# Start-up evictions moved to VectorE, the first seeding behind the last V matmul, and one late weight load four chunks later

## The chip, the cores and the metric

The kernel runs on one core of one Trainium2 chip. A core has five engines, each with an instruction queue of its own that is worked through in order: TensorE (PE, matmuls, with its weight loads shown as PEld), VectorE (DVE), ScalarE (ACT), GpSimd (POOL) and SyncE (SP, which here only issues DMA transfers). ACT and POOL issue DMA transfers too; an issue stands in the same queue as the engine's other work. Matmul results go to PSUM and are copied from there to SBUF ("evicted") by DVE or ACT. The metric is the device time of one execution in microseconds (us), as the median of several.

## The reference

Two independent parts, whose results stand side by side in the output.

```python
def _A_ref(q, k, v, shift_k, ssm_k, ssm_D):            # S = 2048, D = 1024
    k_shift = sum over t < 4 of k_pad[:, t:t + S] * shift_k[:, 3 - t]
    kv = k_shift * v
    y = irfft(rfft(kv, 2 * S) * rfft(ssm_k, 2 * S))[:S] # a long convolution for each channel
    return q * (y + kv * ssm_D)

def _B_ref(x, mem0, Wq, Wk, Wv, Wo, seg_len):           # 32 heads of 128, 8 memory rows, 64 segments of 32
    mem = mem0
    for s in range(64):
        h = concatenate([mem, x[32 * s:32 * s + 32]])   # 40 rows of 1024
        q, k, v = h Wq, h Wk, h Wv                      # each weight 1024 x 4096
        p = softmax(mask(q k^T * scale))
        o = (p v) Wo                                    # 4096 x 1024
        mem = o[:8]
        outs.append(o[8:])
```

The 64 segments of part B depend on each other through `mem`.

## The kernel before

**Part A** works in three stages: stage 1 makes the shifted product and the first transform, stage 2 (34 units) multiplies the spectra, stage 3 (16 units of y_ps matmuls, an `ot` multiplication on DVE by q, and an output store) transforms back. After each unit of stages 2 and 3 a hook `fill()` is called, which works off a piece of part B's preparation. `units[0]` counts these calls, so it is 34 from the last unit of stage 2 on.

**Preparation of part B.** For the last eight rows of all segments at once, K and Q are made by four dense blocks (`dense`, L616; 16 groups of eight kb_ps matmuls each) and V by two halves of 16 groups (vb_ps, L763). Each group ends in one PSUM tile of the pool `ps0`, which has two, and is evicted by `evac` (L608): two of three by ACT, the third by DVE. A dense block collects in a `stage` tile and goes to the DRAM tensor REC by four stores of 512 KB, issued from ACT's queue (L651). V goes to VBD in eight stores, also from ACT's queue (L766): in its first half from one tile with room for four blocks (`vst`), in its second half from `pair` tiles, of which there are two for four blocks. REC and VBD rows are 256 bytes long in these stores.

**Weights.** They don't all fit in SBUF. Most are resident (Wmid, Wres, Wmore, Wlate, pw, and one called Wring), the others are streamed for each segment from the copy WS through a ring of five slots. All these loads stand in SP's queue in the order of the program; `fetch` (L713) issues the next ring load as soon as `done` (L860) frees a slot. Some resident chunks can be loaded only late, when their place is no longer used by the preparation: `place_late`. Wring is one of them. Its place is that of a `pair` tile, and `done` issues its load at the second streamed chunk of segment 0. Two ring slots lie on the transposed X, which the V matmuls read to the last, and one on the other `pair` tile.

**The segments.** Each projects K, Q and V of its 32 first rows (acc, L938), makes scores, softmax and the attention output, and projects that (yacc, L1029). Before the first segment comes the seeding: the record of segment 0 is loaded from REC (L880), Y is loaded from mem0 (L903), both from POOL's queue; a matmul of zeros clears the score bank SB (L904), the mask is copied into it by DVE (`seed_scores`, L908 and L909), and Y is transposed by PE (`fill_mem`, L885) and copied into the record's tile by DVE (L892).

**Order.** Inside `tc.manual_schedule()`, from L896 on, instructions keep the order of the program. Ahead of it a scheduler puts each engine's instructions in order by its own estimate of when they are ready. An instruction that depends on little may so be drawn ahead: the SB matmul and the eight transposes of the first `fill_mem` stand among the V matmuls in PE's queue, after the second and after the third group. `tc.issue_after(x)` keeps what is traced inside it behind x on x's engine.

Of the kernel before, what the change touches and what calls it, by code (L numbers as in the profile page):

```python
# [30 lines left out]
WO_COPY = 29  # L31
Q_LOAD = (10, 13, 16, 19)
X_LOAD = 1
RING = 5

PITCH = 2048
# [384 lines left out]
def b_kernel(ctx: ExitStack, tc, x, mem0, Wq, Wk, Wv, Wo, outb, n_seg, run_a):  # L421
    nc = tc.nc
# [27 lines left out]
    def dram_chunk(ch):  # L450
        m, a, g = ch
        return Wo_v[a] if m == 3 else W_v[m][a, g]

    def dst_view(ap, ch):
        return ap.rearrange("p (hh d) -> p hh d", hh=2) if ch[0] == 3 else ap

    def stream_src(ch):
        return WS[ring_order.index(ch), :, 0:2048]
# [14 lines left out]
    ident = const.tile([128, 128], BF, name="ident")  # L473
# [7 lines left out]
    def xbt(kc):  # L481
        return XBT[kc // 4][:, kc % 4]
# [3 lines left out]
    def pair():  # L486
        turns["pair"] ^= 1
        return base.tile([128, 2048], BF, tag=f"wring{2 + turns['pair']}", name="pair")
# [7 lines left out]
    def pw(k=None):  # L496
        if k is None:
            k = pw_next[0] % 8
            pw_next[0] += 1
        return pring.tile([128, 2048], BF, tag=f"pw{k}", name="pw")  # L500
# [48 lines left out]
    def make_xbt(su):  # L549
        xb = x.rearrange("(tb s t) d -> tb s t d", s=16, t=SEG)  # L550
        for tb in range(4):
            X_sb = pair()[:, 0:1024]
            with tc.issue_after(su[X_LOAD + tb].ins):
                nc.sync.dma_start(X_sb, xb[tb, :, NX:SEG, :])
# [9 lines left out]
    def group(m, g, temps={}, which=range(8), ws=None, eng=nc.sync, held=False):  # L564
        ws = ws or [None] * 8
        for kc in which:
            ch = (m, kc, g)
            if ch in res:
                got.append(eng.dma_start(res[ch], dram_chunk(ch)))
                ws[kc] = res[ch]  # L570
            else:
                t = temps[ch]() if ch in temps else pw()
                got.append(eng.dma_start(t[:], dram_chunk(ch)))
                if ch in streamed:
                    copies.append((stream_src(ch), t[:]))
                ws[kc] = t[:]
        while copies and not held:
            copied.append(nc.gpsimd.dma_start(*copies.pop(0)))
        return ws
# [4 lines left out]
    def x_load(b):  # L584
        t = base.tile([128, 2048], BF, tag="wring2", name="X_sb")
        x_loads.append(nc.sync.dma_start(t[:].rearrange("p (b d) -> p b d", b=2),
                                         x[b * 128:(b + 2) * 128, :].rearrange("(b p) d -> p b d", b=2)))
        loaded[b], loaded[b + 1] = t[:, 0:1024], t[:, 1024:2048]

    def x_block(b):  # L590
        X_sb = loaded.pop(b)
        if b % 2 == 0:
            t = base.tile([128, 2048], BF, tag="wring3", name="xt")
            xts[b], xts[b + 1] = t[:, 0:1024], t[:, 1024:2048]
        tp = ps0.tile([128, 1024], BF, tag="ps0", name="xt_ps")
        for kc in range(8):
            nc.tensor.transpose(tp[:, kc * 128:(kc + 1) * 128], X_sb[:, kc * 128:(kc + 1) * 128], ident[:])
        xt = xts.pop(b).rearrange("p (s k t) -> p s k t", s=4, k=8)
        rows = tp[:].rearrange("p (k j t) -> p j k t", k=8, j=4)
        nc.vector.tensor_copy(xt[:, :, :, NM:SEG], rows[:, :, :, 0:NX])  # L600
        nc.vector.tensor_copy(xt[:, :, :, 0:NM], rows[:, :, :, NX:SEG])
        rec_stores.append(nc.gpsimd.dma_start(REC[:, 4 * b:4 * b + 4, 0:256], xt.rearrange("p s k t -> p s (k t)")))
# [3 lines left out]
    flip = [0]  # L606

    def evac(dst, src):  # L608
        flip[0] += 1
        if flip[0] % 3:  # L610
            nc.scalar.copy(dst, src)
        else:
            nc.vector.tensor_copy(dst, src)
# [35 lines left out]
    def store():  # L649
        if stores:  # L650
            nc.scalar.dma_start(*stores.pop(0))  # L651

    units = [0]
# [3 lines left out]
    def q1_load(kc, k, ins):  # L657
        res[1, kc, 1] = pw(k)[:]
        with tc.issue_after(ins):
            group(1, 1, which=[kc], ws=q1, held=True)  # L660

    def fill(behind=None):
        store()
        n = units[0]
        units[0] += 1
        if n == 0:
            x_load(0)
        if n >= WO_COPY and wo_copies:
            ch = wo_copies.pop(0)
            with tc.issue_after(rec_stores[-1].ins):  # L670
                nc.gpsimd.dma_start(dst_view(stream_src(ch), ch), dram_chunk(ch))
        if n in Q_LOAD:
            i = Q_LOAD.index(n)
            q1_load(kept_q1[i][1], 4 + i, behind.ins)
        if n > 5 and n % 2 and copies:
            with tc.issue_after(rec_stores[-1].ins):
                copied.append(nc.gpsimd.dma_start(*copies.pop(0)))
        if n % 3 == 2 and blocks:
            b = blocks.pop(0)
            x_block(b)  # L680
            if b % 2 and blocks:
                x_load(b + 1)
        if n >= 34 or n % 3 != 2:
            next(rest, None)

    run_a(ps0, pw, slot16, stage1_done, fill)
# [5 lines left out]
    def more(i):  # L692
        return wres3.tile([128, 2048], BF, tag=f"Wmore{i}", name="Wmore")
# [5 lines left out]
    order_s = [ch for ch in order if ch in streamed]  # L699
# [5 lines left out]
    now = [0]  # L705
# [31 lines left out]
    with c0p:  # L737
        temps = dict(zip(v_temp, homes_v))
        wv = [group(2, 0, temps), None]
        for _ in rest:  # L740
            store()
        wv[1] = group(2, 1, temps)
        for i, ch in enumerate(v_temp):
            if i >= 2:
                home = (lambda i=i: more(i)) if i < len(v_temp) - 2 else (lambda k=i - len(v_temp) + 4: pw(k))
                at_hand[ch] = (wv[ch[2]][ch[1]], home)
        while stores:
            store()
        with tc.issue_after(got[-1].ins):
            for _ in range(2):  # L750
                fetch()
        n_k = len(own[0, 0])
        late = late[n_k:-2] + late[4:n_k] + late[:4] + late[-2:]
        for g in range(2):
            ws = wv[g]
            if g == 0:
                vsts = slot16([128, 4, 4, 512], BF, "vst")
            for tb in range(4):
                vst = vsts[:, tb] if g == 0 else pair()[:].rearrange("p (c w) -> p c w", c=4)
                for c in range(4):  # L760
                    ps = ps0.tile([128, 512], F32, tag="ps0", name="vb_ps")
                    for kc in range(8):
                        nc.tensor.matmul(ps[:], lhsT=xbt(kc)[:, 16 * tb:16 * tb + 16, :].rearrange("p s t -> p (s t)"),  # L763
                                         rhs=ws[kc][:, c * 512:(c + 1) * 512], start=(kc == 0), stop=(kc == 7))
                    evac(vst[:, c, :], ps[:])
                nc.scalar.dma_start(  # L766
                    VBD[16 * tb:16 * tb + 16, :, :, :, g * 128:(g + 1) * 128].rearrange("s t c i e -> (s t) (c i) e"),
                    vst.rearrange("p c (i e) -> p (c i) e", i=4))
            if g == 0:
                with tc.issue_after(got[-1].ins):  # L770
                    place_late(4, stage_home)
                    for i in [*range(len(v_temp) - 2, n_more), *range(len(v_temp) - 2)]:
                        place_late(1, lambda: more(i))
                    place_late(1, lambda: pw(2))
                    place_late(4, stage_home)
        assert len(late) == len(at_hand) + 1
# [10 lines left out]
    SB = ps_s.tile([128, 512], F32, name="SB")  # L787
# [72 lines left out]
    def done(ch):  # L860
        if now[0] == 0 and ch in at_hand:
            place_late(1, at_hand[ch][1])
        elif ch in streamed and (now[0] == 0 or ch not in kept):
            if now[0] == 0 and ch in kept:
                keep(ch)
            free.append(live.pop((now[0], ch))[0])
            if now[0] == 0 and ch == order_s[1]:
                place_late(1, lambda: base.tile([128, 2048], BF, tag="wring2", name="Wring"))
            fetch()

# [2 lines left out]
    P_pad = one.tile([128, 5, 64], BF, name="P_pad")  # L873
# [22 lines left out]
    with tc.manual_schedule():  # L896
        for _ in range(RING - 2):
            fetch()
# [2 lines left out]
        nc.vector.memset(Y[:], 0.0)  # L901
        for dh in range(2):
            nc.gpsimd.dma_start(Y[64 * dh:64 * dh + NM, :], mem0[:, dh * 512:(dh + 1) * 512])  # L903
        nc.tensor.matmul(SB[:, 0:320], lhsT=ident[:], rhs=P_pad[:].rearrange("p b k -> p (b k)"), start=True, stop=True,  # L904
                         skip_group_check=True)

        def seed_scores():
            nc.vector.tensor_copy(S[:, 0:4, :], mask[:, 0:1, :].to_broadcast([128, 4, 40]))  # L908
# [284 lines left out]
```

## Time and profile before

| | us |
|---|---|
| three timed runs | 1820.21, 1822.86, 1832.62 |
| their median | 1822.86 |
| the profiled execution: first to last instruction (span) | 1811.8 |
| PE busy in the span | 1701.8 |
| DVE busy | 1010.3 |
| ACT busy | 680.7 |
| POOL busy | 266.7 |

The page gives the span of the profiled execution, not its time with what lies around it. Times in a row of a timeline are counted from the span's start. A timeline row has start, duration of one or of the merged run, engine (with a q where its sequencer issues a DMA), line, operation, output<-inputs, count, and in brackets how long the engine stood idle before it and what ended that. "PEclk" or "granted clock" is the clock that TensorE was allowed, as a share of full speed.

In 40 equal slices of 45.3 us the page shows where the start-up lies: PE's busy tenths are 6 8 8 8 9 9 6 7 5 9 and then 9 to the end, so segments begin to follow each other without gaps in the eleventh.

### The profile page before, as it was taken

The page shows a single profiled execution, that of the slowest core. Times are in us where ns is not written, and L with a number is a line of the kernel's source. Part 1 is how long each engine was busy: PE and PEld are TensorE (multiplying, and loading weights), DVE is VectorE, ACT ScalarE, POOL GpSimd, SP SyncE. Part 2 cuts the span into 40 slices and gives each one's busy share as a digit, 9 for nine tenths or more (in the row PEclk, how much of TensorE's full clock was granted, in tenths as well). Part 3 has the DMA queues.
Part 4 walks back from the last instruction along what each step waited for, and adds up shares of the span by engine and source line. Part 5 has one row for each costly group of instructions (what it writes and reads, how often), then busy time and mean ns, then how long its engine had stood idle before and what let it go on. Part 6 is the DMA issues. An engine that isn't in the chain of part 4 may idle for free.

```text
span 1811.8 us, 71373 instructions
## 1 busy us (share of the span) xinstructions
PE 1701.8 (94%) x30996; PEld 1000.8 (55%) x31028; DVE 1010.3 (56%) x3391; ACT 680.7 (38%) x1195; POOL 266.7 (15%) x499
## 2 busy tenths in 40 slices
PE   6888996759899999999999999999999999999998
PEld 3443322324566666666666666666666666666665
DVE  9927874201455555555555555555555555555555
ACT  6955651112233333333333333333333333333333
POOL 4003341100111111111111111111111111111111
PEclk9999999889999999999999999999999999999999
DMA  9989889997999999999999999999999999999998
GB/s 340 370 305 305 311 258 320 306 335 210 344 365 361 357 350 360 358 363 353 361 356 358 357 352 360 370 358 360 361 355 362 356 358 366 367 363 356 357 358 300
DMA packets 233070, 623.34 MB, mean 344 GB/s; under 512 B 72802, under 2 KB 72946, under 8 KB 232756
## 3 DMA queue, kind: packets, MB, share of 16 engines
q1 hardware_dynamic: 160948, 550.58, 82.4%
q0 software_dynamic: 17056, 45.13, 7.1%
q10 hardware_dynamic: 54752, 23.07, 4.7%
q8 instruction: 243, 3.98, 0.9%
q14 instruction: 71, 0.58, 0.1%
HBM read 563.63 MB, written 57.67 MB: 343 GB/s over the span
## 4 chain that ended last, share of the span: by engine, by line
PE 77%; DMA 9%; DVE 6%; ACT 4%; issue 3%; ACTq 0%; POOL 0%; SPq 0%; another core or an unknown queue 0%; POOLq 0%; DVEq 0%
PE acc L938 33%; PE yacc L1029 24%; PE kb_ps L622 5%; DMA wring<-WS 4%; PE tps L885 3%; PE tps L957 2%; PE vb_ps L763 2%; ACT OT L1019 2%; DMA REC<-stage 2%; DVE mx L972 1%; DVE E L974 1%; ACT s_sb L247 1%; PE OTp L1007 1%; PE s_ps L245 1%; PE SB L963 1%
## 5 line engine op out<-in xcount | busy, mean ns | idle before, releaser
L1029 PEld LDWEIGHTS <-OT 128*64 128x64 bf16 x8255 | 439.1, 109 | 54.6 <-ACT OT L1019 36.9
L938 PEld LDWEIGHTS <-rec 128*32 128x32 bf16 x12288 | 289.4, 96 | 269.3 <-DVE rec L892 35.2
L947 ACT CAST qkv_sb<-acc 128x512 bf16<-128x512 f32 x384 | 225.1, 586 | 352.2 <-PE acc L938 346.9
L938 PE MATMUL acc<-Wres,rec 128*32 128x512 bf16 x3328 | 240.2, 382 | 2.0 <-issue 1.8
L938 PE MATMUL acc<-wring,rec 128*32 128x512 bf16 x2300 | 229.0, 382 | 8.5 <-DMA wring<-WS 7.3
L1029 PE MATMUL yacc<-Wmore,OT 128*64 128x256 bf16 (+1 forms) x2560 | 220.7, 274 | 0.0
L938 PE MATMUL acc<-Wmid,rec 128*32 128x512 bf16 x3072 | 212.1, 379 | 0.5 <-issue 0.3
L1029 PE MATMUL yacc<-wring,OT 128*64 128x256 bf16 x2448 | 194.9, 273 | 2.7 <-DMA wring<-WS 2.5
L1118 ACT CAST Y<-yacc 128x256 bf16<-128x256 f32 x128 | 47.7, 373 | 269.8 <-DVE quarter_b L795 170.8
L938 PE MATMUL acc<-pw,rec 128*32 128x512 bf16 x1796 | 144.7, 380 | 2.0 <-issue 1.9
L795 DVE TENSOR_SCALAR quarter<-OTp 128x256 int32<-128x256 int32 x252 | 99.9, 418 | 74.3 <-ACT OT L1019 74.3
L1019 ACT CAST OT<-OTp 128x640 bf16<-128x640 f32 x128 | 87.4, 683 | 138.5 <-PE OTp L1011 138.5
L1120 POOL DMA_DIRECT2D out_dram<-Y x128 | 63.9, 503 | 496.3 <-ACT Y L1118 496.0
L892 DVE COPY rec<-tps 128x32 bf16<-128x32 bf16 x128 | 22.4, 175 | 193.6 <-PE tps L885 193.6
L938 PE MATMUL acc<-Wlate,rec 128*32 128x512 bf16 x1536 | 117.3, 379 | 0.1
L1057 DVE COPY KT<-tps 128x512 bf16<-128x512 bf16 x64 | 27.2, 425 | 150.8 <-PE tps L885 150.8
L972 DVE TENSOR_REDUCE mx<-SB 128x8 f32<-128x320 f32 x128 | 63.0, 492 | 78.4 <-PE SB L966 78.4
L880 POOL DMA_DIRECT2D rec<-REC x64 | 36.4, 568 | 453.4 <-PE acc L938 437.9
L977 ACT ACTIVATE E<-E 128x320 f32<-128x320 f32 x128 | 60.1, 469 | 78.3 <-DVE E L974 78.3
L1029 PE MATMUL yacc<-Wlate,OT 128*64 128x256 bf16 x1024 | 79.2, 276 | 6.0 <-issue 0.2
L622 PE MATMUL kb_ps<-XBT,pw 128*128 128x512 bf16 x313 | 81.1, 397 | 2.6 <-DMA pw<-in_B_Wk_dram 1.2
L922 POOL COPY KT<-rec 128x128 bf16<-128x128 bf16 x128 | 38.5, 301 | 253.3 <-PE SB L966 253.3
(224 smaller groups left out, 2627.4 us busy)
## 6 DMA issues: line engine op xcount, KB each, us to landing
wring<-WS SPq DMA_DIRECT2D x831, 512.0 KB, 6.0
wring<-WS SPq DMA_DIRECT2D x64, 384.0 KB, 5.4
rec<-REC POOLq DMA_DIRECT2D x64, 192.0 KB, 5.6
SK<-s_sb SPq DMA_DIRECT2D x16, 512.0 KB, 5.3
SU<-s_sb SPq DMA_DIRECT2D x16, 512.0 KB, 5.6
Kg<-SK SPq DMA_DIRECT2D x32, 256.0 KB, 4.1
Ug<-SU SPq DMA_DIRECT2D x32, 256.0 KB, 5.5
REC<-stage ACTq DMA_DIRECT2D x16, 512.0 KB, 12.9
```

The source lines that it names most:

```text
L622: nc.tensor.matmul(ps[:], lhsT=ws[kc][:, hl * 128:(hl + 1) * 128], rhs=xbt(kc).rearrange("p s t -> p (s t)"), start=(kc == 0), stop=(kc == 7))
L795: nc.vector.tensor_scalar(out=dst, in0=src, scalar1=0, scalar2=None, op0=ALU.bitwise_or)
L885: nc.tensor.matmul(dst[e:e + 32, :], lhsT=src[:, e:e + 32], rhs=ident[:], start=True, stop=True, is_transpose=True, tile_position=(0, e))
L922: nc.gpsimd.tensor_copy(KT[:, :, :, 32:40], KBs[:, 128 * g:128 * g + 128].rearrange("p (c i t) -> p i c t", c=4, i=4))
L938: nc.tensor.matmul(self.acc[32 * c:32 * c + 32, :], lhsT=hT[:, ch[1], :], rhs=w[:, 512 * c:512 * c + 512], start=(ch == chs[0]), stop=(ch ...
L947: nc.scalar.copy(sb[:], self.acc[:])
L972: nc.vector.tensor_reduce(out=mx[:], in_=S, op=ALU.max, axis=AX.X)
L977: nc.scalar.activation(E[:], E[:], ACT.Exp, scale=scale)
L1019: nc.scalar.copy(OT[:], o_view)
L1029: nc.tensor.matmul(yacc[f][64 * dh:64 * dh + m, x - o:y - o], lhsT=lhsT, rhs=r, start=(h == (0, 2 * FIRST[-1])[f] and x == o), stop=stop, ...
L1118: nc.scalar.copy(Y[:, 256 * f:256 * f + 256], yacc[f][:, 0:256])
L1120: nc.gpsimd.dma_start(bass.AP(outb.tensor, outb.offset + SEG * s * 2048 + 512 * dh, [[2048, 32], [1, 512]]), Y[64 * dh + NM:64 * dh + 40, :])
```

## The change

Three parts. Evictions by `evac` go to DVE alone once `units[0]` has reached 34, that is from the last unit of stage 2 through stage 3, the last dense blocks and all of V; ACT keeps the stores. The SB matmul of the seeding is put behind the last V matmul on PE, and with it what follows it in the manual order. Wring's load is issued by `done` at the sixth streamed chunk instead of the second.

```diff
+STAGE3 = 34
+LATE_RING = 5
...
     def evac(dst, src):
         flip[0] += 1
-        if flip[0] % 3:
+        if flip[0] % 3 and units[0] < STAGE3:
             nc.scalar.copy(dst, src)
         else:
             nc.vector.tensor_copy(dst, src)
...
-        if n >= 34 or n % 3 != 2:
+        if n >= STAGE3 or n % 3 != 2:
             next(rest, None)
...
                     for kc in range(8):
-                        nc.tensor.matmul(ps[:], lhsT=xbt(kc)[:, 16 * tb:16 * tb + 16, :].rearrange("p s t -> p (s t)"),
-                                         rhs=ws[kc][:, c * 512:(c + 1) * 512], start=(kc == 0), stop=(kc == 7))
+                        v_last = nc.tensor.matmul(ps[:], lhsT=xbt(kc)[:, 16 * tb:16 * tb + 16, :].rearrange("p s t -> p (s t)"),
+                                                  rhs=ws[kc][:, c * 512:(c + 1) * 512], start=(kc == 0), stop=(kc == 7))
                     evac(vst[:, c, :], ps[:])
...
-            if now[0] == 0 and ch == order_s[1]:
+            if now[0] == 0 and ch == order_s[LATE_RING]:
                 place_late(1, lambda: base.tile([128, 2048], BF, tag="wring2", name="Wring"))
             fetch()
...
-        nc.tensor.matmul(SB[:, 0:320], lhsT=ident[:], rhs=P_pad[:].rearrange("p b k -> p (b k)"), start=True, stop=True,
-                         skip_group_check=True)
+        with tc.issue_after(v_last.ins):
+            nc.tensor.matmul(SB[:, 0:320], lhsT=ident[:], rhs=P_pad[:].rearrange("p b k -> p (b k)"), start=True, stop=True,
+                             skip_group_check=True)
```

In the instruction order of the changed program, PE's 256 V matmuls follow each other and the SB matmul and the transposes stand behind them. DVE has ten dense evictions and 32 of V in one row. In stage 3 some y_ps units and dense groups change places on PE. On SP's queue the load of Wring stands behind four more ring loads, three of them full chunks and one of 384 KB.

## The prediction

> **What bounds the kernel now.** I read the page's head first, then the chain of waits in order of time, then the stretches of the start-up, then each engine's timeline between 300 and 490 us.
>
> ```profile
> span 1811.8 us, 71373 instructions
> PE 1701.8 (94%) x30996; PEld 1000.8 (55%) x31028; DVE 1010.3 (56%) x3391; ACT 680.7 (38%) x1195; POOL 266.7 (15%) x499
> ...
> 365.00:380.00 15.00, 4.80 (x20) 1.81 (x19) 1.25 (x3) 0.00 (x0) 1.25 (x3) 0.85 1.08 380
> 380.00:412.00 32.00, 23.56 (x105) 10.34 (x108) 2.94 (x5) 5.62 (x10) 1.45 (x3) 0.80 1.01 313
> 412.00:441.00 29.00, 27.91 (x129) 12.64 (x130) 3.46 (x5) 6.59 (x12) 0.84 (x2) 1.00 0.67 170
> 441.00:475.00 34.00, 25.34 (x461) 15.43 (x459) 13.49 (x50) 8.35 (x14) 0.85 (x2) 0.90 0.91 324
> ...
> 490.00:511.00 21.00, 20.89 (x463) 13.33 (x460) 12.02 (x48) 7.53 (x14) 2.69 (x6) 1.00 0.97 369
> ```
>
> The span stands for one execution; the median of the timed runs is 1822.86, so 11.1 us lie around the span, and I leave them as they are. Columns of a stretch: length, then busy time of PE, weight loads, DVE, ACT and POOL, the granted clock, the DMA share, GB/s. From segment 1 on PE is busy 20.89 of 21 us: nothing to win there, and the change alters no instruction of those 63 segments. What can be won lies before: from 365 to 412 PE works 28.4 of 47 us, and from 441 to 475, segment 0, it works 25.3 of 34.
>
> ```profile
> 364.70 14.02 DMA REC<-stage
> ...
> 380.38 7.82 DMA Y<-in_B_mem_dram
> ...
> 420.96 9.82 DMA VBD<-pair
> ...
> 441.18 5.16 DMA wring<-WS
> ...
> 453.24 4.20 DMA wring<-WS
> ...
> 464.27 6.13 DMA wring<-WS
> ```
>
> These are links of the chain: start, length, what. PE's own rows say what each link costs:
>
> ```profile
> 371.39 0.81 PE L763 MATMUL vb_ps<-Wres,XBT 128*128 128x512 bf16 x3
> 388.33 0.40 PE L885 MATMUL tps<-ident,Y 128*32 128x128 bf16 x8 [16.14 <-DMA Y<-in_B_mem_dram]
> ...
> 441.63 0.38 PE L763 MATMUL vb_ps<-Wres,XBT 128*128 128x512 bf16 x1
> 442.84 0.40 PE L938 MATMUL acc<-wring,rec 128*32 128x512 bf16 x4 [0.83 <-issue]
> ...
> 446.38 0.40 PE L938 MATMUL acc<-wring,rec 128*32 128x512 bf16 x4 [0.24 <-DMA wring<-WS]
> ...
> 457.49 0.62 PE L938 MATMUL acc<-wring,rec 128*32 128x512 bf16 x4 [5.06 <-DMA wring<-WS]
> ...
> 462.95 0.52 PE L1029 MATMUL yacc<-Wlate,OT 128*64 128x256 bf16 x6
> ...
> 470.44 0.63 PE L1029 MATMUL yacc<-wring,OT 128*64 128x256 bf16 x8 [2.53 <-DMA wring<-WS]
> ...
> 475.09 0.40 PE L938 MATMUL acc<-wring,rec 128*32 128x512 bf16 x4
> ```
>
> Three of 32 V groups (eight matmuls each) are done at 372.2; then PE stands 16.14 us, because the seeding's transposes of Y lie next in its order. V ends at 442.0, segment 1 begins at 475.1. Segment 0 thus takes 33.1 us, with 5.06 and 2.53 us of waits for ring chunks.
>
> **Part 1 and 2: evictions on DVE, seeding behind V.** They have to be costed together.
>
> ```profile
> 364.70 15.98 ACTq L651 DMA_DIRECT2D REC<-stage  x4
> 380.80 1.07 ACT L611 CAST vst<-vb_ps 128x512 bf16<-128x512 f32 x2 [16.13 <-DMA REC<-stage]
> ...
> 369.57 0.69 DVE L613 CAST vst<-vb_ps 128x512 bf16<-128x512 f32 x1 [6.51 <-PE vb_ps L763]
> ...
> 394.29 0.69 DVE L613 CAST vst<-vb_ps 128x512 bf16<-128x512 f32 x1 [5.33 <-PE vb_ps L763]
> 399.47 0.69 DVE L613 CAST vst<-vb_ps 128x512 bf16<-128x512 f32 x1 [4.49 <-PE vb_ps L763]
> ```
>
> ACT issues the four REC stores of the last dense block from 364.70 on and is held by them to 380.68; the V evictions behind them in its queue run at 380.80. With two PSUM tiles, V could not have gone on before about 381.4 even without the seeding. So moving the seeding alone frees 7 us of the 16, moving the evictions alone nothing; together they free all of it. DVE needs 0.69 us an eviction, and a V group comes every 1.73 us (three groups from 394.29 to 399.47), so DVE keeps up, and the 0.10 us by which it is slower than ACT (1.07 for two) stays hidden. With no other wait, 29 groups from 372.2 on end at 372.2 + 29 x 1.73 = 422.4, 19.6 us earlier.
>
> What comes late next is not the weights: the last two chunks for the second half of V are issued at 378.81 (row below), and that half would begin at 372.2 + 13 x 1.73 = 394.7. It is the stores.
>
> ```profile
> 378.81 1.00 SPq L569 DMA_DIRECT2D Wres<-in_B_Wv_dram  x2
> ...
> DMA to landing us min/median/max: 14.2/14.2/14.2
> ...
> DMA to landing us min/median/max: 4.0/4.0/4.0
> ...
> VBD<-vst ACTq DMA_DIRECT2D x4, 512.0 KB, 12.6
> ```
>
> The first landing row is the fourth REC store alone (issued at 378.7, so landed at 392.9), the second the VBD store of 435.8, which ran with hardly a load beside it. ACT's DMA queue is passed in order. In the second half of V two `pair` tiles serve four blocks, so the eviction of block 2 waits until the VBD store of block 0, the fifth in the queue, has landed; before, it had landed at 430.8 (the chain's 420.96 link), about when block 2 came to it. Now V runs 16 us sooner but the REC stores do not. Four REC stores took 364.7 to 392.9, 7.0 us each, beside loads. Up to 412 loads fill the DMA (share 1.01, then 0.67: the stretches above), so I take 7.0 us a store from 392.9: 2.7 stores by 412. The other 2.3 run nearly alone at 4.0 us: 9.2 us. The fifth lands at 421. Then comes the eviction (0.7) and six more groups (10.4): V ends at 432, **9.8 us earlier**. Bounds: stores that cost nothing (422.4, 19.6 us) and every store at the median of 12.6 (a rival below).
>
> The seeding itself now lies between V and segment 0.
>
> ```profile
> 370.17 0.32 DVE L908 CAST SB<-mask 128x160 f32<-128x160 bf16 x1
> 370.53 0.33 DVE L909 CAST SB<-mask 128x160 f32<-128x160 bf16 x1
> 388.78 0.17 DVE L892 COPY rec<-tps 128x32 bf16<-128x32 bf16 x1 [17.93 <-PE tps L885]
> ```
>
> Behind the last V matmul stand on DVE the last eviction (0.69), the two mask copies (0.32 and 0.33) and the copy of the transposed Y (0.17), which the first projection needs: with the small gaps 1.7 us instead of the 0.83 before. The SB matmul and the transposes (0.4 us) run beside the eviction. 0.24 us of the difference disappears in the wait at 446.38. Cost: +0.65 us, between 0 (if the ring chunk lands later anyway) and 0.9. Y and the rec load stay where they are on POOL and land 40 us ahead.
>
> **Stage 3.** There the evictions move behind DVE's `ot` multiplications.
>
> ```profile
> 300.93 2.35 DVE L414 TENSOR_TENSOR ot<-y_ps,qt 128x1024 bf16<-128x1024 f32 x2 [5.70 <-DMA out_dram<-ot]
> ...
> 331.86 1.03 PE L407 MATMUL y_ps<-zt,G2h 128*128 128x512 bf16 x2 [9.04 <-DMA zt<-SZ]
> ```
>
> DVE stands 5.70 us for an output store; two dense groups that ACT evicted meanwhile now wait for it, so that the dense block ends some 2 us later, and with it the REC stores and the zt load behind them. Against it, in the changed order a whole dense group (eight matmuls, 1.7 us) stands ahead of the matmuls of 331.86 and fills part of that 9.04 us wait. I take **0**, between 2 us gained and 2 lost.
>
> **Part 3: the late ring chunk.**
>
> ```profile
> 452.80 0.38 SPq L726 DMA_DIRECT2D Wring<-in_B_Wo_dram  x1
> ...
> 484.00 0.39 PE L938 MATMUL acc<-wring,rec 128*32 128x512 bf16 x4
> ...
> 488.12 0.63 PE L1029 MATMUL yacc<-Wlate,OT 128*64 128x256 bf16 x8
> ```
>
> The load of Wring waits at the head of SP's queue until the last VBD store has landed. Behind it stand the ring chunks whose slots are long free; the chain's 453.24 link is the first of them, and PE waits 5.06 us for it. Four chunks later the same wait stands behind those loads. Its slot comes free between 442.84 and 446.38, when the second ring chunk has been used; issued then, it lands 4.2 to 6.1 us later (the links), so by 452.4, when PE asks. So 5.06 go. The stretch after the wait ran at a lower clock: from 457.49 to 462.95 it took 5.46, in segment 1 (484.00 to 488.12) 4.12: 1.3 us go too. The 2.53 us wait stays, since its chunk can only be loaded when its slot frees. Wring itself is an output chunk, used behind 462.95 and long after its new place. Sum: **-6.4 us**; bounds 0 (chunks late for DMA) and -10.
>
> **Sum.** -9.8 + 0.65 + 0 - 6.4 = -15.5 us: span 1796.3, time 1822.9 - 15.5 = **1807.4**.
>
> **Rivals.** *The stores don't bind* (0.20). If ACT's queue moves the eight VBD stores at the alone price of 4.0 us, the fifth lands by 413 and V ends near 423: 19 - 0.65, with part 3 about 25, 1798. For it: ACT's queue has no evictions between its stores any more. Against: four REC rows at 7.0.
>
> ```profile
> GB/s 415 407 406 409 405 420 309 287 249 301 262 400 408 243 45 289 278 369 390 393 384 342 334 282 206 223 101 133 312 196 310 284 190 163 6 0 211 48 156 314
> ```
>
> This line has the DMA rate in 2 us steps from 364 on: 410 GB/s at its fullest, 45 at 392. From 365 to 475 the four stretches above move 31.7 MB (length times rate); at 380 GB/s, the fullest stretch, that is 83 us, and segment 1 could begin at 448, so DMA as a whole would allow this rival.
> [...]
>
> *Stage 3 gives part of it back* (0.14): DVE's stalls for stores and q loads reach PE through the two PSUM tiles, up to twice the 5.70 us row, and V starts as much later: 4 us gained in all, 1819. Against: PE waits for zt there anyway.
>
> *The stores bind all through* (0.06, the other side). At t us a store from 392.9, the sixth, which the last block waits for, lands at 392.9 + 6t, and V ends 4.2 us later. With 5.7 us gained behind V, it is break-even at t = 8.4. At the median of 12.6, V ends at 472.7: 30.7 - 5.7 = 25 us slower, 1848. For it: the VBD row. Against: those stores came 6.9 us apart (four groups) and so overlapped, and the loads beside them thin out at 412.
>
> That the change does nothing would need the moved instructions to stay in place; in the changed program's order V's 256 matmuls stand together and ACT has no eviction left there.
>
> **How the numbers follow.** The forecast case, 10 to 20 us faster, has 0.60. A measurement of this kernel can tell about 1%, 18.2 us. Faster by more: nearly all of the first rival and a fourth of the forecast, 0.33. Slower by more: the last, 0.06. The same: 0.61. The range reaches from the first rival with part 3 at its bound (1798 - 3.6) to the stage-3 rival with stage 3's own bound on top (1819 + 2): 1794 to 1821. It leaves out the last rival, and the edges of the others.
>
> **What would show it.** Right: no PE wait for Y near 372; V's last matmul between 427 and 436 with its longest wait at block 2 of the second half, put down to VBD<-pair; ACT without an eviction of the dense blocks or of V from stage 3 on; Wring issued behind the 384 KB load, with no 9 us gap of SP ahead; the wait of 5.06 below 2. Wrong: V at 422 or past 440, a ring wait in segment 0 as long as before, or any change of the 20.9 us a segment.

## The result and the profile after

| | before | changed |
|---|---|---|
| median of 12 runs, us | 1822.71 | 1812.70 |
| lowest and highest | 1813.22, 1832.62 | 1807.46, 1817.85 |
| span of the profiled execution | 1811.8 | 1805.7 |

The ratio is 0.9946, with a 95% interval of 0.9926 to 0.9965: 6.4 to 13.5 us faster; the forecast was 15.5. In the profiled executions the difference is 6.1 us. The page and the stretches of the start-up, for the changed kernel:

```profile
span 1805.7 us, 71361 instructions
...
PE 1700.6 (94%) x30996; PEld 999.9 (55%) x31028; DVE 1035.2 (57%) x3429; ACT 658.6 (36%) x1157; POOL 266.1 (15%) x499
```

```profile
365.00:380.00 15.00, 13.17 (x60) 5.85 (x60) 5.54 (x8) 0.00 (x0) 1.14 (x2) 1.00 0.98 373
380.00:412.00 32.00, 31.84 (x147) 14.46 (x148) 12.45 (x19) 0.00 (x0) 2.12 (x4) 1.00 1.07 318
412.00:441.00 29.00, 20.04 (x116) 8.34 (x119) 7.54 (x14) 0.00 (x0) 0.84 (x2) 0.88 0.93 266
441.00:475.00 34.00, 26.26 (x528) 16.36 (x520) 13.22 (x50) 9.79 (x17) 2.69 (x6) 0.90 0.92 336
```

From 365 to 412 PE now works 45.0 of 47 us, where it worked 28.4. ACT has no busy time from 365 to 441: its evictions are gone, the DVE column has grown instead. The stretch behind, 412 to 441, has lost 8 us of PE's work, and the DMA share there rose from 0.67 to 0.93. PE's own rows, of the same kernel, say where it now stands:

```profile
305.36 0.59 PE L599 MATMUL xt_ps<-ident,X_sb 128*128 128x128 bf16 x4 [3.88 <-DVE stage L615]
...
338.90 1.87 PE L409 MATMUL y_ps<-zt,G2h 128*128 128x512 bf16 x4 [9.57 <-DMA zt<-SZ]
...
369.99 0.81 PE L765 MATMUL vb_ps<-Wres,XBT 128*128 128x512 bf16 x3
...
423.99 0.58 PE L765 MATMUL vb_ps<-pw,XBT 128*128 128x512 bf16 x1 [6.85 <-DVE pair L615]
...
434.30 0.38 PE L765 MATMUL vb_ps<-pw,XBT 128*128 128x512 bf16 x1 [0.97 <-DVE pair L615]
...
437.75 0.30 PE L907 MATMUL SB<-P_pad,ident 128*128 128x320 bf16 x1
...
439.37 0.40 PE L941 MATMUL acc<-wring,rec 128*32 128x512 bf16 x4 [1.09 <-DVE rec L894]
...
462.00 1.07 PE L1032 MATMUL yacc<-wring,OT 128*64 128x256 bf16 x8 [4.79 <-DMA wring<-WS]
...
467.35 0.63 PE L1032 MATMUL yacc<-wring,OT 128*64 128x256 bf16 x8 [1.57 <-DMA wring<-WS]
...
470.43 0.40 PE L941 MATMUL acc<-wring,rec 128*32 128x512 bf16 x4
```

The wait of 16.14 us for Y is gone. In its place stands 6.85 us at block 2 of V's second half: DVE's eviction there waits for a `pair` tile, and so for a VBD store. V begins at 369.99 instead of 363.89 and ends near 437.9 instead of 442.0. Segment 0 (439.37 to 470.43) takes 31.1 us where it took 32.25: the wait of 5.06 us for a ring chunk is gone from the projections and is back, with 4.79 us, in the output projection. SP's queue of this kernel, the DMA issues only:

```profile
437.08 8.20 SPq L724 DMA_DIRECT2D wring<-WS  x7
446.50 0.32 SPq L722 DMA_DIRECT2D wring<-WS  x1
454.64 0.38 SPq L728 DMA_DIRECT2D Wring<-in_B_Wo_dram  x1
455.12 0.42 SPq L724 DMA_DIRECT2D wring<-WS  x1
```

The gap of 8 us ahead of Wring has not shrunk with its new place; it stands behind the 384 KB load now. What it waits for is the last VBD store, issued at 438.7. The time from issue to landing of that one store, first in the kernel before (issued at 442.8), then in the changed one:

```profile
DMA to landing us min/median/max: 9.9/9.9/9.9
```

```profile
DMA to landing us min/median/max: 15.9/15.9/15.9
```

### The profile page after: what moved, and what is told of

Read it like the earlier page. It is cut to its first block, busy times and chain, and to the rows that moved or that the text cites. A ratio compares the mean times of both kernels' runs of the same rounds, so it can differ in the third digit from the quotient of the medians.

```text
span 1805.7 us, 71361 instructions
## 1 busy us (share of the span) xinstructions
PE 1700.6 (94%) x30996; PEld 999.9 (55%) x31028; DVE 1035.2 (57%) x3429; ACT 658.6 (36%) x1157; POOL 266.1 (15%) x499
## 4 chain that ended last, share of the span: by engine, by line
PE 76%; DMA 10%; DVE 7%; ACT 4%; issue 3%; ACTq 1%; POOL 0%; SPq 0%; POOLq 0%; DVEq 0%
PE acc L941 32%; PE yacc L1032 23%; DMA wring<-WS 5%; PE kb_ps L624 4%; PE tps L887 3%; PE vb_ps L765 2%; PE tps L960 2%; ACT OT L1022 2%; DVE mx L975 2%; DVE E L977 2%; PE s_ps L247 1%; DMA REC<-stage 1%; DMA out_dram<-ot 1%; ACT s_sb L249 1%; PE ks_ps L285 1%
```

## The experiments

Each kernel was timed against the kernel before on the same chip, in five rounds. An edit is shown against the changed kernel, or against the kernel that its heading or a note beside it names. For all of them the traces give three stretches, in us: V, from its first matmul to the end of its last; segment 0, from its first projection matmul to that of segment 1; and the rest, up to the last instruction. They tell the parts apart better than the time, since the rest alone varies from 1335.3 to 1347.0 between executions whose segments differ in nothing, or nearly nothing.

| kernel | V begins | V takes | segment 0 takes | ratio to before, 95% interval |
|---|---|---|---|---|
| before | 363.9 | 78.1 | 32.3 | |
| changed | 370.0 | 67.9 | 31.1 | 0.9946 (0.9926 to 0.9965) |
| e1 seeding moved alone | 368.0 | 76.2 | 31.0 | 0.9987 (0.9971 to 1.0003) |
| e2 evictions alone (see there) | 367.0 | 67.8 | 29.9 | 0.9954 (0.9937 to 0.9970) |
| e3 late ring chunk alone | 367.1 | 79.3 | 32.1 | 1.0001 (0.9985 to 1.0017) |
| e4 all but late ring chunk | 369.5 | 66.9 | 33.1 | 0.9955 (0.9936 to 0.9974) |
| e5 V's evictions, seeding early | 366.0 | 77.3 | 33.3 | 1.0004 (0.9984 to 1.0025) |
| e6 DVE's evictions in V only | 364.4 | 68.0 | 32.1 | 0.9928 (0.9902 to 0.9954) |
| e7 Wring two chunks later still | 364.1 | 66.6 | 31.7 | 0.9948 (0.9929 to 0.9967) |
| e8 second half's stores from POOL | 370.3 | 80.2 | 39.0 | 1.0063 (1.0044 to 1.0081) |
| e9 as e6, last store in four | 367.0 | 67.8 | 28.2 | 0.9914 (0.9893 to 0.9934) |
| e10 as e6, late loads from POOL | 366.0 | 67.8 | 29.7 | 0.9952 (0.9935 to 0.9970) |
| e11 as e6, V rows of 4 KB | 366.1 | 65.7 | 27.8 | 0.9915 (0.9894 to 0.9936) |
| e12 as e9, Wring early | 367.2 | 68.2 | 29.2 | 0.9912 (0.9889 to 0.9935) |

**e1: the seeding moved, nothing else.**

```diff
-        if flip[0] % 3 and units[0] < STAGE3:
+        if flip[0] % 3:
...
-LATE_RING = 5
+LATE_RING = 1
```

> The changed kernel with the evictions shared by ACT and DVE as before and Wring at the second chunk as before: only the seeding is moved. The prediction's step: PE's 16.14 us wait for Y becomes a wait of about 9 for an eviction that stands behind ACT's REC stores, and the stores then bind V as in the prediction: between 3 and 7 us faster than before, 1816 to 1820. Rival (stores bind all): no change within 2 us. Rival (the seeding was the whole loss): 10 us faster, as the changed kernel.

1817.93 against 1821.31 us; by the ratio 2.4 us faster, between 5 faster and none; the midpoint lies just below the 3 to 7 us expected. PE's waits in V, in e1:

```profile
385.50 1.44 PE L765 MATMUL vb_ps<-Wres,XBT 128*128 128x512 bf16 x3 [9.47 <-ACT vst L613]
...
403.35 0.81 PE L765 MATMUL vb_ps<-Wres,XBT 128*128 128x512 bf16 x3 [3.02 <-ACT vst L613]
```

The first wait is as long as the prediction's step has it: the transposes no longer hold PE, the eviction behind ACT's REC stores does, and 6.7 us are freed. But the next eviction that stands behind a store in ACT's queue takes 3.02 of them back, and V is only 1.9 us shorter.

**e2: the evictions on DVE, nothing else.**

```diff
-        with tc.issue_after(v_last.ins):
-            nc.tensor.matmul(SB[:, 0:320], ...
+        nc.tensor.matmul(SB[:, 0:320], ...
...
-LATE_RING = 5
+LATE_RING = 1
```

> The kernel before with evictions on DVE alone from the last unit of stage 2 on. The prediction: nothing moves in V, since the seeding's wait ends no earlier, and nothing in stage 3: 0 within 2 us. Rival drawn from the changed kernel's trace (the first V group begins at 369.99 instead of 363.89): stage 3 ends 6 us later, REC stores and the loads of V weights with it, so 4 to 6 us slower, 1827 to 1829.

1811.81 us, as fast as the changed kernel: against both expectations. The row of the zero matmul in e2 tells why:

```profile
434.64 0.30 PE L907 MATMUL SB<-P_pad,ident 128*128 128x320 bf16 x1
```

It stands behind V's last matmul, though nothing in the source puts it there any more. With the evictions on DVE the scheduler no longer draws the seeding ahead (its own estimates of V, which differ with the evicting engine, are presumably why). So e2 is not one part alone, its PE order is that of the changed kernel, and it repeats e4. The explicit placement in the change decides nothing here; the evictions bring the order along.

**e3: the late ring chunk alone.**

```diff
-            if now[0] == 0 and ch == order_s[1]:
+            if now[0] == 0 and ch == order_s[5]:
```

(against the kernel before)

> The kernel before with Wring issued at the sixth streamed chunk. The prediction: 6.4 us faster (5.06 of wait and 1.3 of low clock), 1816. Rival drawn from the changed kernel's trace (the last VBD store took 15.9 us from issue to landing instead of 9.9, beside eight ring loads instead of four): the loads let past the store slow it, Wring and the loads behind it wait for it all the same, and the wait of PE moves into the output projection: 0 to 2 us faster, 1821 to 1823, with a PE wait of 4 to 5 us on a ring chunk in the output projection of segment 0.

No change: ratio 1.0001, 3 us either way. The rival holds in each of its steps. The last wait for a ring chunk in the projections of e3, the longest in its output projection and, in the second fence, the landing of its last VBD store:

```profile
457.21 0.40 PE L941 MATMUL acc<-wring,rec 128*32 128x512 bf16 x4 [0.36 <-DMA wring<-WS]
...
469.28 1.06 PE L1032 MATMUL yacc<-wring,OT 128*64 128x256 bf16 x8 [4.75 <-DMA wring<-WS]
```

```profile
DMA to landing us min/median/max: 14.8/14.8/14.8
```

The 5.06 us of the kernel before are gone from the projections, and 4.75 us are new in the output projection. The store that SP waits for takes 14.8 us instead of 9.9, with eight ring loads beside it and not four.

**e4: all but the late ring chunk.**

```diff
-LATE_RING = 5
+LATE_RING = 1
```

> The changed kernel with Wring at the second streamed chunk as before. The prediction: evictions and seeding give 9.2 us and the ring chunk the other 6.4, so this kernel lies 6 us above the changed one, near 1819. Rival: the ring chunk gave 0 to 2 us, so this kernel is at 1812 to 1815, and PE waits 4 to 6 us for a ring chunk ahead of the output projection instead of in it.

1813.51 us, 0.9955 against the changed kernel's 0.9946: the rival. With e1 and e3 this places the gain: seeding and evictions together, 8.2 us (5 to 12) by the ratio; the ring chunk nothing that five rounds can tell.

**e5: the evictions with the seeding where it was.** Leaving V's first eviction to ACT keeps the scheduler's old order, with the zero matmul behind two and the transposes behind four V groups.

```diff
-        if flip[0] % 3 and units[0] < STAGE3:
+        if flip[0] % 3 and not (v_n[0] >= 2):
...
+                    v_n[0] += 1
                     evac(vst[:, c, :], ps[:])
```

(and without the placement of the seeding, Wring as before)

> The kernel before with the evictions of V's groups 2 to 32 on DVE; the zero matmul and the transposes of the seeding stay among the first V groups on PE (behind two and four groups). Of the changed kernel's parts only the evictions are here. Theory (prediction: moving the evictions alone frees nothing): PE still stands for Y until about 390, a wait of 10 to 17 us, and the time is that of the kernel before within 3 us. Rival (evictions on DVE are the gain, wherever the seeding lies): 8 to 10 us faster, 1811 to 1814.

1822.47 against 1822.11 us: no change. The wait for Y in e5:

```profile
390.97 0.41 PE L889 MATMUL tps<-ident,Y 128*32 128x128 bf16 x8 [14.32 <-DMA Y<-in_B_mem_dram]
```

V's first eviction, left to ACT, waits for the REC stores there as well, but these let ACT go at 382.9; the wait for Y outlasts it. DVE's queue is free all that time, and it helps nothing. With e1 the pair is complete: 2.4 us for the one part, nothing for the other, 8.2 for both.

**e6: DVE's evictions from the first V group on, stage 3 as before.**

```diff
-        if flip[0] % 3 and units[0] < STAGE3:
+        if flip[0] % 3 and not in_v[0]:
...
+        in_v[0] = True
         for g in range(2):
             ws = wv[g]
```

> The changed kernel with DVE's evictions from the first V group on only; stage 3 and the dense blocks are evicted by ACT and DVE as in the kernel before. Theory (the changed kernel's first V group began at 369.99 and waited 3.9 us in stage 3 for an eviction behind DVE's stall for an output store; that costs): V begins 2 to 5 us earlier, 2 to 4 us faster than the changed kernel, 1808.5 to 1811. Rival (the prediction's 0 for stage 3: PE waits for zt there anyway): 1812 to 1814.

1808.01 us, ratio 0.9928 to the changed kernel's 0.9946: 3.3 us better by the midpoints, with intervals that overlap. V begins at 364.4. Over all traces, five kernels with DVE's evictions in stage 3 (changed, e2, e4, e7, e8) begin V at 364.1 to 370.3, 368.2 in the mean; the other nine at 363.9 to 368.0, 366.2 in the mean. The means lie 2.0 us apart, and single executions scatter by more, so what stage 3 costs is not shown. All five have the wait of the 305.36 row, of 3.9 to 4.4 us, and none of the nine has it; yet e7, with 4.4 us of it, begins V at 364.1, so later waits can take it up.

**e7: Wring two chunks later still.**

```diff
-LATE_RING = 5
+LATE_RING = 7
```

> The changed kernel with Wring at the eighth streamed chunk, so that two more ring loads go ahead of it. Theory A (the wait is Wring's own, for its tile): the ring load that PE waited 4.79 us for no longer stands behind it: 4 to 5 us faster than the changed kernel, 1808. Theory B (the last VBD store holds SP's queue in another way: DMA completions are counted in a few semaphores used in turn, the eighth load after the store has to take over the store's, and is held until it lands): the same gap of 7 to 8 us on SP's queue stays, now ahead of a ring load, and the time is the changed kernel's within 2 us.

1813.76 us, the changed kernel's time: theory B. SP's queue in e7, and the landing of its last VBD store, which was issued at 431.5:

```profile
429.88 7.59 SPq L724 DMA_DIRECT2D wring<-WS  x7
438.69 0.32 SPq L722 DMA_DIRECT2D wring<-WS  x1
446.24 0.32 SPq L724 DMA_DIRECT2D wring<-WS  x1
...
447.09 0.46 SPq L728 DMA_DIRECT2D Wring<-in_B_Wo_dram  x1
```

```profile
DMA to landing us min/median/max: 14.7/14.7/14.7
```

Between 439 and 446.24 SP issues nothing, though what stands next is an ordinary ring load and Wring only behind it. It goes out as the store lands (431.5 + 14.7 = 446.2). In the trace each transfer has a completion counter, and SP's and ACT's transfers take eight of them in turn. In the changed kernel Wring, issued at 454.64, has the counter of the last store, which was issued at 438.68 and landed at 454.58; in e7 a ring load stands in Wring's place in the turn. In both the transfer that stands eighth behind the store in this turn waits for it, 7.8 and 7.2 us behind SP's issue before it, and SP's queue with it.

**e8: the four stores of V's second half from POOL**, each in four pieces of 512 rows.

```diff
-                nc.scalar.dma_start(
-                    VBD[16 * tb:16 * tb + 16, :, :, :, g * 128:(g + 1) * 128]...
+                if g == 1:
+                    for c in range(4):
+                        nc.gpsimd.dma_start(
+                            VBD[16 * tb:16 * tb + 16, :, c, :, g * 128:(g + 1) * 128]...
```

> The changed kernel with the four VBD stores of V's second half issued from POOL's queue, each in four pieces. Theory (V waits at block 2 of its second half since the fifth store stands behind four REC and four VBD stores in ACT's queue): the 6.85 us wait falls below 3, the last store and Wring come sooner: 3 to 8 us faster than the changed kernel, 1805 to 1810. Rival (the stores are bound by the DMA engines that all queues share, not by their order in ACT's queue): the fifth store lands at 421 to 424 as before, 1811 to 1814; or worse, if POOL's issues hold the loads of VBs and rec: 1815 to 1820.

1833.09 us, 11 us slower than the kernel before: worse than the worst expectation. POOL's queue in e8, and PE's second wait in V:

```profile
437.79 0.76 POOL L770 DMA_DIRECT2D VBD<-pair  x1 [1.98 <-issue]
440.48 0.75 POOL L770 DMA_DIRECT2D VBD<-pair  x1 [1.93 <-issue]
443.25 0.76 POOL L770 DMA_DIRECT2D VBD<-pair  x1 [2.02 <-issue]
```

```profile
443.98 0.59 PE L765 MATMUL vb_ps<-pw,XBT 128*128 128x512 bf16 x1 [7.12 <-DVE pair L615]
```

The pieces go out one at a time, 2.7 us apart at best, so that a block takes 10.9 us at best (four pieces) where V makes one in 6.9 (four groups of 1.73). V waits 7.79 and then 7.12 us and ends at 450.4. The theory on the order of ACT's queue was not tested by this: POOL's own pace took its place.

**e9: e6 with the last store in four**, each part behind its own eviction, still from ACT.

```diff
+                    step = 1 if g == 1 and tb == 3 else 4
+                    if c % step == step - 1:
+                        a, b = c + 1 - step, c + 1
+                        nc.scalar.dma_start(
+                            VBD[16 * tb:16 * tb + 16, :, a:b, :, g * 128:(g + 1) * 128]...
```

> The kernel with V's evictions alone on DVE (the best so far, 1808.0), with the last VBD store cut into four, each issued behind its own eviction. Theory (the last store, 14 to 16 us from issue to landing beside the ring loads, holds a completion count that SP's queue has to take over, and with it the ring loads that PE waits for in the output projection): the last quarter lands by about 441 instead of 448 of that kernel's trace, SP's gap of 7 us shrinks below 2, PE's waits of 4.32 and 1.57 us to 2 or less together: 3 to 5 us faster, 1803 to 1805. Rival (the DMA engines are full in segment 0, share 0.9 and over, so the ring loads come no sooner whatever holds the queue): the waits stay within 1 us in sum, 1807 to 1809.

1806.42 us, not the 1803 to 1805 expected. Segment 0 takes 28.2 us instead of 32.1, 3.9 less, about as the theory has it; the time came down by 1.4 per mille (2.6 us), which the intervals do not separate from e6. What is left in e9, and the landings of the four parts:

```profile
458.87 1.07 PE L1037 MATMUL yacc<-wring,OT 128*64 128x256 bf16 x8 [3.01 <-DMA wring<-WS]
```

```profile
DMA to landing us min/median/max: 2.0/7.2/10.6
```

The last quarter, issued at 435.6, still needs 10.6 us for 128 KB and lands at 446.2, not the 441 expected. It is shorter, but it runs beside the same loads.

**e10: e6 with the late loads from POOL's queue.**

```diff
-        nc.sync.dma_start(dst_view(ap, ch), dram_chunk(ch))
+        late_eng[0].dma_start(dst_view(ap, ch), dram_chunk(ch))
...
+                late_eng[0] = nc.gpsimd
-                with tc.issue_after(got[-1].ins):
+                with tc.issue_after(copied[-1].ins):
                     place_late(4, stage_home)
...
+                late_eng[0] = nc.sync
```

> The kernel with V's evictions alone on DVE (1808.0), with the resident chunks that are loaded while V runs (Wlate, Wmore, one pw) issued from POOL's queue instead of SP's. Theory (the fifth VBD store was ready at 403, but ACT could issue it only at 408.18, when the load whose completion count it takes over had landed; from POOL the loads use other counts): the fifth store is issued by 404 and lands by 414, the 7.32 us wait of V at block 2 falls to 4 or less: 3 to 5 us faster, 1803 to 1805. Rival (the stores' pace is set by ACT's queue and the DMA engines): the fifth store lands at 417 to 419 as before, 1807 to 1809. Third (POOL issues more slowly or holds the load of VBs or rec, or a late chunk comes too late for segment 0): slower, over 1810.

1813.13 us; the ratio is 0.9952 to e6's 0.9928, with intervals that overlap. It is no faster, and the theory falls. ACT's queue in e10, and the wait of V:

```profile
382.85 25.68 ACTq L772 DMA_DIRECT2D VBD<-vst  x4
408.62 26.50 ACTq L772 DMA_DIRECT2D VBD<-pair  x4
```

```profile
420.57 0.59 PE L769 MATMUL vb_ps<-pw,XBT 128*128 128x512 bf16 x1 [7.81 <-DVE pair L616]
```

With the loads' counters out of the way the four stores of the first half still take 25.7 us to issue, of which the fourth alone holds ACT for 8.1 (from 400.5), and the fifth goes out at 408.62, not by 404. From the landing of the last REC store to that of the fifth VBD store it is 21.6 us here, 22.9 in the changed kernel, 23.4 in e6: with these counters or without them a store takes 4.3 to 4.7 us in the mean.

**e11: e6 with VBD laid out by halves of V**, so that a store writes rows of 4 KB.

```diff
-    VBD = dram.tile([n_seg, 8, 4, 4, 256], BF, name="VBD")
+    VBD = dram.tile([2, n_seg, 8, 4, 4, 128], BF, name="VBD")
...
-                    VBD[16 * tb:16 * tb + 16, :, :, :, g * 128:(g + 1) * 128]...
+                    VBD[g, 16 * tb:16 * tb + 16].rearrange("s t c i e -> (s t) (c i e)"),
...
-            nc.gpsimd.dma_start(VBs[:].rearrange("p g e -> p (g e)"), VBD[s]...
+            for g in range(2):
+                nc.gpsimd.dma_start(VBs[:, g, :], VBD[g, s].rearrange("t c i e -> (c i) t e"))
```

> The kernel with V's evictions alone on DVE (1808.0), with VBD laid out by halves of V, so that a store of the same 512 KB writes 128 rows of 4 KB instead of 2048 of 256 bytes; in return each segment reads VBs in two loads with rows of 256 bytes instead of one with 512. Theory (the stores bind V since their small rows take the DMA engines' time: share 1.05 to 1.15 at 250 to 320 GB/s where weight loads reach 400): a store lands within 6 us of its issue, the 7.32 us wait of V at block 2 falls below 2 and V ends near 425 instead of 432; the last store lands by 437 instead of 448 and the waits for ring chunks in segment 0's output projection (4.32 and 1.57) lose 3 us or more: 8 to 12 us faster, 1796 to 1800, if a segment stays at 20.9 us. Rival (the engines are filled by the loads, whatever the rows of the stores are): the wait stays above 4, 1804 to 1808. Third (the smaller reads cost each segment 0.1 to 0.3 us): 6 to 19 us of it are given back, 1804 to 1818.

1807.31 us. The stretch of V's second half, in e6 and then in e11:

```profile
412.00:431.00 19.00, 10.80 (x43) 4.54 (x43) 4.28 (x7) 0.00 (x0) 0.84 (x2) 0.82 0.91 243
```

```profile
412.00:431.00 19.00, 13.54 (x55) 5.68 (x54) 4.75 (x7) 0.00 (x0) 0.83 (x2) 0.82 0.73 287
```

More bytes (287 against 243 GB/s) in less of the DMA engines' time (0.73 against 0.91): the small rows do cost it. PE's waits in e11 and the landing of its last store:

```profile
419.62 0.58 PE L767 MATMUL vb_ps<-pw,XBT 128*128 128x512 bf16 x1 [5.41 <-DVE pair L616]
...
456.41 0.63 PE L1035 MATMUL yacc<-wring,OT 128*64 128x256 bf16 x8 [2.53 <-DMA wring<-WS]
```

```profile
DMA to landing us min/median/max: 8.9/8.9/8.9
```

The last store lands in 8.9 us instead of e6's 14.7, and segment 0 takes 27.8 us. V's wait falls to 5.41 only, against the theory's 2. What holds the fifth store there, issued at 412.40, is not shown: the 0.73 is a mean of 19 us and doesn't tell how full the DMA engines were just then. In the changed kernel that store was issued at 413.42, behind the landing, at 413.34, of a Wmore load with the same completion counter, so the cause taken away in e10 may bind here too. The two together were not tried, and this stays open. Start-up ends at 461.1 instead of 465.9, 4.8 us sooner, but the rest takes 1347.0 us, the longest of all, against e6's 1341.0. Whether that is the price of the smaller reads, about 0.1 us a segment, or scatter, one trace can't tell.

**e12: e9 with Wring at the second chunk again.**

```diff
-LATE_RING = 5
+LATE_RING = 1
```

> The kernel with the last store in four (1806.4) with Wring back at the second streamed chunk. Theory (the late ring chunk pays only once the last store is short: in that kernel's trace it left segment 0 at 27.4 us, against 30.5 to 31.5 with the store whole): with Wring early the ring loads stand behind it until the last quarter has landed, segment 0 takes 30 us or more and the time is 2 to 4 us more, 1808.5 to 1810.5. Rival (the split store is all of it; with four ring loads fewer beside them the quarters land sooner, and the order of Wring is worth nothing here either): segment 0 at 27 to 28.5 us, 1805.5 to 1807.5.

1807.91 us lies between the two ranges expected; the ratio is 0.9912 to e9's 0.9914, so in the time the rival holds. Segment 0 takes 1 us more, with the waits shared out the other way:

```profile
449.41 0.40 PE L946 MATMUL acc<-wring,rec 128*32 128x512 bf16 x4 [3.38 <-DMA wring<-WS]
...
461.26 0.97 PE L1037 MATMUL yacc<-wring,OT 128*64 128x256 bf16 x8 [2.50 <-DMA wring<-WS]
```

e9, e11 and e12 lie at 0.9912 to 0.9915, the lowest of all; each is 0.3% below the changed kernel by the midpoint, with an interval that overlaps its own at the edge. DVE's evictions in V alone, with the last store in four, is the version to keep, though its time is not separated from that of e6.

## Why the prediction was right, and where not

The time, 1812.7, lies in the range, and the direction is right; the size is two thirds of the forecast, and 15.5 us lie outside the measured interval. The range is 27 us wide, so that the time lies in it says little of the steps:

- **What bounds the kernel.** Right: all that the profiled executions differ by ahead of segment 1 is 4.7 us (475.09 to 470.43), and behind it 1.4 us. Wrong is the note that 11.1 us lie around the span. The runs of the changed kernel give time and span of the same executions, and 1.8 us lie between (1807.46 and 1805.7). The profiled execution of the kernel before was a quick one; the forecast, a difference, was not touched by it.
- **Evictions and seeding free the 16 us only together.** Shown by e1, e5 and e4.
- **V ends 9.8 us sooner, held by the fifth VBD store.** Right in place, and in size by luck. V takes 10.2 us less in the changed kernel, and 10.1 to 11.5 less in e2, e4, e6 and e7; the changed kernel's V ends only 4.1 us sooner, since it begins 6.1 later. e7 has V begin where the kernel before has it (364.1) and ends V at 430.7, forecast 432. The terms inside were off, against each other. In e7 the last REC store landed at 393.5 (378.9 + 14.6; forecast 392.9), the fifth VBD store 22.9 us behind it (406.7 + 9.7) instead of 28.1, so a store beside the loads costs 4.6 us and not first 7.0, then 4.0. From there V took 14.3 us instead of 11.1, most of it because PE ran at a low clock right behind its stand of 6 to 7 us, at 0.63 in e7 from 417.2 to 424; the changed kernel's stretch behind its wait has a granted clock of 0.61:

```profile
424.00:430.00 6.00, 5.95 (x17) 2.22 (x18) 1.31 (x3) 0.00 (x0) 0.64 (x2) 0.61 1.05 299
```

- **The seeding, +0.65 us.** Right: from V's end to the first projection it is 0.83 us before and 1.46 after.
- **Stage 3, 0 between -2 and +2.** Not settled: +2.0 by the mean starts of V, +3.3 by e6's time, neither clear of the scatter. The wait itself is shown, in the place named: an eviction stands behind an `ot` multiplication, which waits for an output store (the 3.88 us row at 305.36). How much of it the waits for zt behind it hide stays open.
- **The late ring chunk, -6.4 us.** This is the step that failed. The ring loads ahead of Wring did land in time for the projections, though they took 5.2 to 8.7 us (changed, e3, e6 and e7) and not 4.2 to 6.1. What the sum took as fixed was the landing of the store that everything behind Wring waits for. The four loads that now pass run beside that store and stretch it from 9.9 us (9.8 to 10.3 in before, e1, e2, e4 and e5, with Wring early) to 14.7 to 15.9 (changed, e3, e6 and e7, with Wring late). The 5.06 us come back as 4.3 to 4.8 in the output projection (changed, e3, e6; in e7 in several pieces), and segment 0 is as long as before: 31.1 to 32.1 in the latter four against 29.9 to 33.3 in the former five.

With the last term at 0 and stage 3 anywhere in its bounds, the prediction's own sum is -7.2 to -11.2 us; measured are -6.4 to -13.5.

Of its own signs, those on the wait for Y, on V's longest wait and on ACT's evictions came as named. V ended at 437.9, behind the 427 to 436 that were to show it right. Two of the signs came out against part 3: SP's gap ahead of Wring stayed, with 7.8 us, and segment 0 kept a ring wait of 4.79. Of the rivals, *the stores don't bind* falls by the 6.85 us that V waits for a store, *the stores bind all through* by the 4.6 us a store, and a gain of only 4 us lies outside the measured interval.

What a store of 512 KB takes beside the loads is shown by its landings alone: 4.0 us nearly alone and 9.9 beside four ring loads (before), 14.7 to 15.9 beside eight (changed, e3, e6 and e7), and with rows of 4 KB, Wring late as well, 8.9 (e11). How the DMA engines share their time between a store and the loads, no run shows.

## What to carry to other kernels

When a wait stands at the head of a queue, ask what releases it, and whether what you let past it slows just that: here four loads moved ahead of a wait for a store made the store some 5 us later, as much as there was to gain. Two obstacles in a row on different engines (a matmul early in PE's order, an eviction behind a store in ACT's queue) show their worth only when both go; take each away alone and look at the order that the scheduler makes of it before believing the split. If a store decides when the next stage may load, it is worth making its last part small or its rows long: segment 0 took 27.8 to 29.2 us in e9, e11 and e12, against 29.6 to 33.3 where ACT stored whole blocks with short rows.

## What the runs showed that was not expected

- A store from ACT held a load on SP: the transfer that stands eighth behind the last VBD store in the turn of the completion counters waited until it had landed, Wring for 7.8 us in the changed kernel, a ring load for 7.2 in e7.
- Stores of 512 rows from POOL went out one by one, 2.7 us apart at best (e8), though POOL itself is busy for 0.76 us with each.
- A quarter of a store, 128 KB in 256-byte rows, took up to 10.6 us beside ring loads (e9), as long as the whole store took beside four of them (9.8 to 10.3).
- The engine of the evictions changed the order of matmuls: with all of V's evictions on DVE the scheduler put the seeding behind V by itself (e2, the zero matmul at 434.64).
